# Reordering the fifth pair, one in-product of the next pairs, and some loads of an attention and feed-forward kernel

## The chip, the cores and the metric

The kernel runs on one core of one Trainium2 chip. The metric is the device time of one execution in microseconds (us), as the median of several runs; lower is better.

## The reference

Eight batches of eight heads of attention with a T5 bias, then a feed-forward block over the heads put side by side.

```python
scores = scale * np.matmul(q, k.transpose(0, 1, 3, 2))      # q, k, v: (8, 8, 576, 64)
scores = scores + bias.transpose(2, 0, 1)[None, :, :, :]    # a function of |i - j| and the head
scores = scores - np.max(scores, axis=-1, keepdims=True)
attn = np.exp(scores)
attn = attn / (np.sum(attn, axis=-1, keepdims=True) + 1e-09)
attn_out = np.matmul(attn, v)
...
x = attn_out.transpose(0, 2, 1, 3).reshape(B * S, H * D)    # (4608, 512)
h = x @ w_in                                                # w_in: (512, 2048)
g = np.maximum(0.01 * h, h)
return g @ w_out                                            # w_out: (2048, 512)
```

## The kernel before

The work of attention is cut into 32 pairs: pair n is batch n // 4 and two of its heads, `p = n % 4`. The feed-forward block is cut into nine blocks of 512 tokens; each has 16 in-products (four matmuls of 512 columns into one PSUM bank, then a leaky ReLU, `leaky`, on ScalarE or VectorE) and 16 quarters of out-products. These pieces are put between the steps of the pairs, so that TensorE has work while ScalarE and VectorE are at the attention. The order on each engine is the order in which the code is written (`manual_schedule`); semaphores are set by a framework, and so is the choice of a buffer within a pool.

The steps of a pair, by the names that the text uses:

- `transpose_q(n)`, `transpose_k(n)`: twelve (early pairs) or six transposes on TensorE into a bank of `ps_m`, then a copy to SBUF (L294 for q, L298 for k). From pair 9 on the transposes are made by DMA (`turn_by_dma`, L265) from rows that VectorE lays out (`pair_rows`, L257).
- `score(n, u)`: matmuls of keys and queries into one of the two buffers of `ps_s` (L316; u = 5, the last 64 keys, L319 and L320; u = 4, the edges, into `ps_o`, L309), then the exponential on ScalarE (L329, L336, L332). Below, third and fourth score are u = 2 and 3, fifth score is u = 5, and edge scores are u = 4.
- `band(n, u)`: VectorE multiplies the exponentials near the diagonal by the bias (L352).
- `av_tails(n)` and `av(n, e)`: the products with the values for head e (L365, L376), then `divide` on VectorE (reciprocal L385, product L387) into the tile `opair`. In later pairs `av_phase` (L411) does both heads in halves of the rows.
- `x_transposes(n)`: `opair` is turned into columns of `xT`, on TensorE (L437, copy L438) or by a DMA from SyncE's queue (L427).
- `piece_in` / `ffn_in` (L463, or L623 in halves) and `piece_out` / `ffn_out` (L504, L623): the pieces of the feed-forward block. `moe(k)` issues up to k in-products, `slot()` one, or two quarters, as planned for the pair.

The pool `ps_m` has two banks, which transposes and feed-forward pieces share.

Pairs 0 to 3 fill the pipeline with attention alone. Pair n = 4, the fifth, is written out by hand and has the first four in-products: one, two and one, at three places. Pairs 5 and 6 are pairs with only in-products (`room["only"]`), run by the general loop. From pair 8 on most pairs run `body_in_halves`.

Loads from HBM are issued on POOL's queue, in order. `load_qk(b, h0, h1)` brings q and k of some heads of a batch, `load_v_part` chunks of v, `load_w_in(half)` half of `w_in`. In the steady part `loads(n)` brings the next batch's data. It first has POOL copy one element of an earlier pair's `opair` (`tick`, L785), so that the loads behind it start only when that pair is divided:

```python
nc.gpsimd.tensor_copy(out=tick, in_=ops_[n - 2][0:1, 0, 0:1])
```

`loads(n)` with `p == 1` brings q and k of the next batch's upper heads and the first chunk of v.

Of the kernel before, what the change touches and what calls it, by code (L numbers as in the profile page):

```python
# [37 lines left out]
def kernel(  # L38
# [10 lines left out]
    nc = tc.nc  # L49

    B, H, S, D = q.shape
# [57 lines left out]
    def load_qk(b, h0, h1):  # L109
        i = b % NBUF  # L110
        for src, dst in ((q, qn[i]), (k, kn[i])):
            nc.gpsimd.dma_start(
                out=dst[0:RQ, h0:h1, :, :].rearrange("r h c d -> r h (c d)"),
                in_=src[b, h0:h1, :, :].rearrange("h (r c) d -> r h (c d)", c=NC),
            )

    def load_v_part(b, chunks, h0=0, h1=H):
        for c in chunks:
            nc.gpsimd.dma_start(  # L119
                out=vn[b % NBUF][:, c, h0:h1, 0:D],  # L120
                in_=v[b, h0:h1, c * P : (c + 1) * P, :].rearrange("h s d -> s h d"),
            )
# [56 lines left out]
    for j, (u, lo, w, m) in enumerate(groups):  # L179
# [5 lines left out]
        out=ub[:, C0 - BAND + 1 : C0],  # L185
# [42 lines left out]
    load_qk(1, 0, H // 2)  # L228
    load_v_part(0, range(NJ), 4, H)
    clear_v(nc.gpsimd, 1)  # L230
    load_qk(1, H // 2, H)

    def load_w_in(half):
        o = slice(half * (DF // 2), (half + 1) * (DF // 2))
        nc.gpsimd.dma_start(out=w_in_sb[:, :, o], in_=moe_w_in[:, o].rearrange("(c p) f -> p c f", p=P))
# [55 lines left out]
    def transpose_q(n):  # L291
        qt = qts[n] = qt_pool.tile([P, S], BF16, name="qt")
        copy = nc.scalar.copy if n <= n_pairs else nc.vector.tensor_copy
        copy(out=qt[:, 0:S].rearrange("p (r c) -> p r c", c=NC), in_=turned_pair(n, 0))  # L294

    def transpose_k(n):
        kt = kts[n] = kts_[n % 2]
        nc.vector.tensor_copy(out=kt[:, 0:S].rearrange("p (r c) -> p r c", c=NC), in_=turned_pair(n, 1))  # L298
        apart(kt)
# [69 lines left out]
    def av(n, e):  # L369
        b, p = items[n]  # L370
        at = at_[n % 2]
        ps = outs[n][e][:, 0 : (NJ + 1) * (D + 1)].rearrange("p (i d) -> p i d", d=D + 1)
        for ic in range(NJ + 1):
            for c in range(NJ):
                o = (e * NJ + c) * S + ic * P
                nc.tensor.matmul(ps[:, ic, :], lhsT=at[:, o : o + P], rhs=vn[b % NBUF][:, c, 2 * p + e, :],  # L376
                                 start=False, stop=(ic == NJ and c == NJ - 1))
        divide(n, (e,))
# [14 lines left out]
    def fence(sooner):  # L393

        f = nc.sync.nop(nofuse=True)  # L395
        tc.add_manual_dep(f.ins, sooner.ins.name, ended, reason="behind the last products of these rows")
        return f
# [243 lines left out]

    def body_in_halves(n, kinds):

        loads(n)
        turns = rows_ahead(n) if by_dma(n + 1) else []
        score(n, 0)
        av_tails(n - 1)
        last = fence(av_phase(n - 1, 0))
        score(n, 1)
        T, s = made["out"], at_piece["out"]  # L650
        if kinds[0] == "out":
            one, two = open_piece("out", (T, s)), open_piece("out", (T, s + 4))
        else:
            one, two = open_piece("in"), open_piece("out")
        phase = side_by_side(one, two)
        phase(0, 0, 1)
        av_phase(n - 1, 1, last)
        late_q = n == 2 * n_pairs
        if n + 1 < N and not late_q:
            transpose_q(n + 1)  # L660
        band(n, 0)
        divide(n - 1, range(2))
        if late_q:
            transpose_q(n + 1)
        last = fence(phase(0, 1, n_cc))
        score(n, 2)
        score(n, 3)
        phase(1, 0, n_cc, last)
        band(n, 1)
        if n + 1 < N:  # L670
            transpose_k(n + 1)
        score(n, 4)
        if kinds[0] == "in":
            one[2]()
        late = [n - 1]
        if x_by_dma(n - 1):
            x_transposes(late.pop())
        for m in turns:
            turn_by_dma(m)
        while stores:  # L680
            o, y = stores.pop(0)
            nc.sync.dma_start(out=o, in_=y)
        band(n, 2)
        if kinds[0] == "out":
            outs_pm[T] = one[0]
            ffn_out(T, s + 1)
            band(n, 4)
            score(n, 5)
            band(n, 5)
            ffn_out(T, s + 2)  # L690
            ffn_out(T, s + 3)
            for m in late:
                x_transposes(m, "o0")
                finished(m)
            outs_pm[T] = two[0]
            for part in range(5, 8):
                ffn_out(T, s + part)
            at_piece["out"] = (s + 8) % n_fc
            made["out"] += at_piece["out"] == 0
            return  # L700
        piece_out()
        band(n, 4)
        score(n, 5)
        band(n, 5)
        piece_out()
        piece_out()
        for m in late:
            x_transposes(m, "o1")
            finished(m)
        room["left"] -= 5  # L710
        moe(room["left"], 0)
# [56 lines left out]

    tick = per.tile([1, 1], BF16, name="tick")

    def loads(n):

        b, p = items[n]
        if n == 0:
            load_w_in(0)
            load_v_part(1, range(NJ))
            load_v_tail(1)
            load_w_in(1)
            load_w_out(0)
        elif n == 2:  # L780
            load_qk(2, 0, H // 2)
            load_w_out(1)
        if b < 1 or p < 1 or b > B - 2:
            return
        nc.gpsimd.tensor_copy(out=tick, in_=ops_[n - 2][0:1, 0, 0:1])  # L785
        if p == 1:
            load_qk(b + 1, H // 2, H)
            load_v_part(b + 1, (0,))
        elif p == 2:
            load_v_part(b + 1, (1, 2, 3))  # L790
        else:
            load_v_tail(b + 1)
            if b + 2 < B:
                load_qk(b + 2, 0, H // 2)
# [17 lines left out]
    def score(n, u):  # L812
        exp(n, u, qk_mm(n, u))
# [44 lines left out]
    n = n_pairs  # L858
# [2 lines left out]
    band(n - 1, 4)  # L861
    av_tails(n - 1)
    av(n - 1, 0)
    score(n, 2)
    av(n - 1, 1)
    score(n, 3)
    transpose_k(n + 1)
    x_transposes(n - 1)
    finished(n - 1)
    band(n, 0)  # L870
    band(n, 1)
    score(n, 5)
    room["left"] = 4
    moe(1)
    band(n, 2)
    transpose_q(n + 1)
    score(n, 4)
# [6 lines left out]
    for n in range(n_pairs + 1, N + 1):  # L884
        live = n < N
        more = n + 1 < N
        if x_by_dma(n - 2):
            finished(n - 2)
        plan(n)
        kinds = two_kinds(n)  # L890
        if kinds:
            body_in_halves(n, kinds)
            continue
        if live:
            begin(n)
            ps_a, ps_b = qk_mm(n, 0), qk_mm(n, 1)
            exp(n, 0, ps_a)
            exp(n, 1, ps_b)
        av_tails(n - 1)
        av(n - 1, 0)  # L900
        first = live and by_dma(n + 1)
        if first:
            band(n, 0)
        if more:
            transpose_q(n + 1)
        if live and not first:
            band(n, 0)
            turn_ahead(n)
        slot()
        av(n - 1, 1)  # L910
        if live and not room["only"]:
            band(n, 1)
        if more:
            transpose_k(n + 1)
        slot(True)
        if live:
            ps_a, ps_b, ps_c = qk_mm(n, 2), qk_mm(n, 3), qk_mm(n, 4)
            exp(n, 2, ps_a)
        x_transposes(n - 1)
        while stores:  # L920
            o, y = stores.pop(0)
            nc.sync.dma_start(out=o, in_=y)
        if not x_by_dma(n - 1):
            finished(n - 1)
        if not live:
            break
        if room["only"]:
            band(n, 1)
        band(n, 2)
        if room["only"]:  # L930
            if not by_dma(n + 2):
                pair_rows(n + 2)
            exp(n, 3, ps_b)
            moe(2)
            exp(n, 4, ps_c)
            score(n, 5)
            T, f = step("in")
            room["left"] -= 1

            def last_bands():  # L940
                band(n, 5)
                band(n, 4)

            leaky(T, f, ffn_in(T, f), True, last_bands)
            moe(room["left"])
            continue
        block = moe_block()
        next(block)
        exp(n, 3, ps_b)
        next(block)  # L950
        exp(n, 4, ps_c)
        if can("out"):
            next(block)
        band(n, 4)
        ps_a = qk_mm(n, 5)
        exp(n, 5, ps_a)
        band(n, 5)
        for _ in block:
            pass
# [31 lines left out]
```

## Time and profile before

| | |
|---|---|
| time, median of 3 runs | 372.75 us (372.66 to 373.42) |
| time of the profiled execution | 372.35 us |
| its span, first to last instruction | 370.6 us |
| granted TensorE clock | 1.000 |
| TensorE busy | 356.3 us (96%) |
| ScalarE busy | 245.4 us (66%) |
| VectorE busy | 192.9 us (52%) |
| POOL busy | 76.4 us (21%) |

All times below come from the one profiled execution. In a row of the timeline the first number is the start in us from the span's start, the second the duration of the group, then engine, line, operation, the tile written and the tile read, the shapes and the count; idle time before it and what ended it stand in brackets. PE is TensorE's matmuls, DVE is VectorE, ACT is ScalarE, SPq and POOLq are queues of DMA issues. Matmuls are pipelined: the next one starts long before the last one's end, so the distance between starts tells more than the duration.

### The profile page before, as it was taken

The page shows a single profiled execution, that of the slowest core. Times are in us where ns is not written, and L with a number is a line of the kernel's source. Part 1 is how long each engine was busy: PE and PEld are TensorE (multiplying, and loading weights), DVE is VectorE, ACT ScalarE, POOL GpSimd, SP SyncE. Part 2 cuts the span into 40 slices and gives each one's busy share as a digit, 9 for nine tenths or more (in the row PEclk, how much of TensorE's full clock was granted, in tenths as well). Part 3 has the DMA queues.
Part 4 walks back from the last instruction along what each step waited for, and adds up shares of the span by engine and source line. Part 5 has one row for each costly group of instructions (what it writes and reads, how often), then busy time and mean ns, then how long its engine had stood idle before and what let it go on. Part 6 is the DMA issues. An engine that isn't in the chain of part 4 may idle for free.

```text
span 370.6 us, 10507 instructions
## 1 busy us (share of the span) xinstructions
PE 356.3 (96%) x4453; PEld 187.7 (51%) x4496; DVE 192.9 (52%) x502; ACT 245.4 (66%) x382; POOL 76.4 (21%) x118
## 2 busy tenths in 40 slices
PE   6889999999999999999999999999999999999996
PEld 2455555555555555555555554555555544444443
DVE  4688687777757576666755566665553200200000
ACT  5998887478847787777877776777777365055111
POOL 8754431233023303330233023100000000000000
DMA  8999999999379989986799399532111000110122
GB/s 105 188 193 183 207 203 115 196 180 160 56 103 165 140 114 116 153 133 131 97 122 143 87 102 152 112 72 62 46 48 50 28 30 0 59 56 0 72 72 85
DMA packets 104358, 40.17 MB, mean 108 GB/s; under 512 B 83184, under 2 KB 98808, under 8 KB 104312
## 3 DMA queue, kind: packets, MB, share of 16 engines
q0 software_dynamic: 53696, 18.36, 50.9%
q1 hardware_dynamic: 49320, 19.06, 26.9%
q10 hardware_dynamic: 1296, 2.10, 1.5%
q8 instruction: 35, 0.57, 0.7%
q14 instruction: 11, 0.09, 0.1%
HBM read 37.68 MB, written 9.45 MB: 127 GB/s over the span
## 4 chain that ended last, share of the span: by engine, by line
PE 87%; ACT 4%; DMA 3%; DVE 3%; issue 2%; POOL 0%; ACTq 0%; DVEq 0%; POOLq 0%
PE pm L463 28%; PE pm L504 27%; PE pm L623 8%; PE ps_s L316 8%; PE ps_o L411 6%; PE ps_o L376 4%; DMA xT<-opair 2%; ACT at L329 2%; PE ps_s L319 2%; PE ps_o L365 1%; DVE opair L387 1%; PE ps_tx L437 1%; PE ps_q L309 1%; DMA kn<-in_k_dram 1%; PE pm L497 1%
## 5 line engine op out<-in xcount | busy, mean ns | idle before, releaser
L329 ACT ACTIVATE at<-ps_s 128x1024 bf16<-128x1024 f32 x128 | 124.6, 1028 | 25.6 <-PE ps_s L316 25.5
L476 ACT ACTIVATE gt<-pm 128x512 bf16<-128x512 f32 x138 | 82.9, 605 | 70.3 <-PE pm L463 69.4
L463 PE MATMUL pm<-xT,w_in_sb 128*128 128x512 bf16 x490 | 117.2, 379 | 1.1
L504 PE MATMUL pm<-w_out_sb,gt 128*128 128x512 bf16 x452 | 105.9, 379 | 3.3 <-issue 3.0
L352 DVE TENSOR_TENSOR at<-at,hk 128x768 bf16<-128x768 bf16 (+3 forms) x160 | 70.8, 454 | 58.0 <-ACT at L329 33.7
L463 PEld LDWEIGHTS <-w_in_sb 128*128 128x128 bf16 x508 | 47.8, 98 | 54.5 <-issue 0.7
L504 PEld LDWEIGHTS <-gt 128*128 128x128 bf16 x476 | 43.5, 98 | 49.5
L316 PE MATMUL ps_s<-qt,kt 64*128 64x512 bf16 x256 | 43.3, 380 | 3.6 <-ACT at L329 3.0
L623 PE MATMUL pm<-w_out_sb,gt 64*128 64x512 bf16 x168 | 42.2, 376 | 0.0
L517 DVE COPY y<-pm 128x512 f32<-128x512 f32 x28 | 19.4, 691 | 40.9 <-PE pm L504 38.1
L623 PE MATMUL pm<-xT,w_in_sb 64*128 64x512 bf16 x136 | 37.7, 376 | 0.4 <-DMA xT<-opair 0.4
L119 POOL DMA_DIRECT2D vn<-in_v_dram x32 | 29.9, 939 | 10.4 <-PE ps_s L316 8.1
L387 DVE TENSOR_TENSOR opair<-ps_o,rcp 128x320 bf16<-128x320 f32 x64 | 29.7, 488 | 1.6
L785 POOL COPY tick<-opair 1x1 bf16<-1x1 bf16 x18 | 3.5, 194 | 129.2 <-DVE opair L387 129.2
L411 PE MATMUL ps_o<-vn,at 64*128 64x65 bf16 x1520 | 29.5, 190 | 0.0
L411 PEld LDWEIGHTS <-at 64*128 64x128 bf16 x1520 | 27.1, 94 | 4.3 <-SPq L395 3.0
L316 PEld LDWEIGHTS <-kt 64*128 64x128 bf16 x256 | 11.6, 94 | 25.4 <-issue 16.5
L336 ACT ACTIVATE at<-ps_s 128x576 bf16<-128x576 f32 x32 | 21.8, 683 | 0.2 <-PE ps_s L320 0.2
L332 ACT ACTIVATE at<-ps_q 128x256 bf16<-128x256 f32 x64 | 21.4, 396 | 0.3 <-PE ps_q L309 0.2
L385 DVE RECIPROCAL rcp<-ps_o 128x5 f32<-128x5 f32 x64 | 10.0, 182 | 21.6 <-PE ps_o L376 18.3
L376 PE MATMUL ps_o<-vn,at 128*128 128x65 bf16 x520 | 20.1, 194 | 0.0
L376 PEld LDWEIGHTS <-at 128*128 128x128 bf16 x520 | 17.9, 98 | 3.5 <-issue 0.7
(66 smaller groups left out, 254.4 us busy)
## 6 DMA issues: line engine op xcount, KB each, us to landing
out_dram<-y SPq DMA_DIRECT2D x28, 256.0 KB, 3.6
qn<-in_q_dram POOLq DMA_DIRECT2D x14, 288.0 KB, 5.9
kn<-in_k_dram POOLq DMA_DIRECT2D x14, 288.0 KB, 7.0
vn<-in_v_dram POOLq DMA_DIRECT2D x28, 128.0 KB, 6.3
w_in_sb<-in_moe_w_in_dram POOLq DMA_DIRECT2D x2, 1024.0 KB, 12.4
w_out_sb<-in_moe_w_out_dram POOLq DMA_DIRECT2D x2, 1024.0 KB, 15.7
out_dram<-y ACTq DMA_DIRECT2D x7, 256.0 KB, 2.0
qn<-in_q_dram POOLq DMA_DIRECT2D x4, 144.0 KB, 4.4
```

The costliest lines, as they stand in the source:

```text
L119: nc.gpsimd.dma_start(out=vn[b % NBUF][:, c, h0:h1, 0:D], in_=v[b, h0:h1, c * P : (c + 1) * P, :].rearrange("h s d -> s h d"),)
L316: nc.tensor.matmul(ps[:, e, :], lhsT=kt[r, u * P : (u + 1) * P], rhs=qt[r, 0:512], start=True, stop=True)
L329: nc.scalar.activation(at[:, :, u, 0:512], ps, AF.Exp, scale=scale)
L336: nc.scalar.activation(at4[:, 0:S], ps.rearrange("p e i -> p (e i)")[:, 0:S], AF.Exp, scale=scale)
L352: nc.vector.tensor_tensor(out=o, in0=o, in1=m, op=ALU.mult)
L376: nc.tensor.matmul(ps[:, ic, :], lhsT=at[:, o : o + P], rhs=vn[b % NBUF][:, c, 2 * p + e, :], start=False, stop=(ic == NJ and c == NJ - 1))
L387: nc.vector.tensor_tensor(out=opair[:, :, e * D : (e + 1) * D], in0=ps[:, :, 0:D], in1=rcp.to_broadcast([P, NJ + 1, D]), op=ALU.mult)
L411: m = nc.tensor.matmul(outs[n][e][:, ic * (D + 1) : (ic + 1) * (D + 1)], lhsT=at[halves[r], o : o + P], rhs=vn[b % NBUF][halves[r], c, 2 * ...
L463: nc.tensor.matmul(pm, lhsT=w_in_sb[:, c, f * P : (f + 1) * P], rhs=xT[c][:, t0 : t0 + TT], start=(c == 0), stop=(c == n_cc - 1))
L476: nc.scalar.activation(g, pm, AF.Prelu, bias=0.0, scale=1.0, alpha=0.01)
L504: nc.tensor.matmul(pm, lhsT=gt[:, f, ts * P : (ts + 1) * P], rhs=w_out_sb[:, f, :], start=(f == 0), stop=(f == n_fc - 1))
L623: m = nc.tensor.matmul(pm, lhsT=w[halves[r]], rhs=x[halves[r]], start=(k == 0 and c == 0), stop=(low is not None and k == 1 and c == n_cc ...
```

## The change

Four edits. In the fifth pair both value products stand ahead of the third score, and the output transposes, the fifth score and the first in-product ahead of the key transposes. On POOL's queue the first half of `w_in` is loaded ahead of q and k of the upper heads of batch 1. In pairs 5 and 6 the first in-product stands behind the second value product. In `body_in_halves` a pair with `p == 1` (n = 9, 13, 17, 21, 25) calls `loads` after its division, and the tick reads the `opair` of pair n - 1 in place of n - 2.

```diff
     clear_v(nc.gpsimd, 1)
-    load_qk(1, H // 2, H)
...
     def body_in_halves(n, kinds):
-        loads(n)
+        late_loads = items[n][1] == 1
+        if not late_loads:
+            loads(n)
...
         if late_q:
             transpose_q(n + 1)
+        if late_loads:
+            loads(n, 1)
         last = fence(phase(0, 1, n_cc))
...
-    def loads(n):
+    def loads(n, behind_pair=2):
         b, p = items[n]
         if n == 0:
             load_w_in(0)
+            load_qk(1, H // 2, H)
             load_v_part(1, range(NJ))
...
-        nc.gpsimd.tensor_copy(out=tick, in_=ops_[n - 2][0:1, 0, 0:1])
+        nc.gpsimd.tensor_copy(out=tick, in_=ops_[n - behind_pair][0:1, 0, 0:1])
...
     av_tails(n - 1)
     av(n - 1, 0)
+    av(n - 1, 1)
     score(n, 2)
-    av(n - 1, 1)
     score(n, 3)
-    transpose_k(n + 1)
     x_transposes(n - 1)
     finished(n - 1)
+    score(n, 5)
     band(n, 0)
-    band(n, 1)
-    score(n, 5)
     room["left"] = 4
     moe(1)
+    transpose_k(n + 1)
+    band(n, 1)
     band(n, 2)
     transpose_q(n + 1)
     score(n, 4)
...
-        slot()
+        if not room["only"]:
+            slot()
         av(n - 1, 1)
+        if room["only"]:
+            slot()
```

## The prediction

> **What bounds the kernel now.** I read the page first: busy shares, then the chain that ended last.
>
> ```profile
> span 370.6 us, 10507 instructions
> ...
> PE 356.3 (96%) x4453; PEld 187.7 (51%) x4496; DVE 192.9 (52%) x502; ACT 245.4 (66%) x382; POOL 76.4 (21%) x118
> ...
> PE 87%; ACT 4%; DMA 3%; DVE 3%; issue 2%; POOL 0%; ACTq 0%; DVEq 0%; POOLq 0%
> ```
>
> TensorE is busy 96% of the span and 87% of the chain. A change is therefore worth what it adds to or takes from TensorE's idle time, so I went to the list of TensorE's waits for a wait that one of the four edits could touch, and found one in the steady part, late in the kernel:
>
> ```profile
> PE pm L623 <- DMA xT<-opair: 0.4, 1, 0.4
> ```
>
> The other edits lie in the fifth to seventh pairs (n = 4, 5, 6), and for these I read the timeline engine by engine. TensorE in the fifth pair:
>
> ```profile
> 31.08 0.39 PE L316 MATMUL ps_s<-qt,kt 64*128 64x512 bf16 x2
> 31.41 0.79 PE L376 MATMUL ps_o<-vn,at 128*128 128x65 bf16 x20
> 32.13 0.39 PE L316 MATMUL ps_s<-qt,kt 64*128 64x512 bf16 x2
> 32.45 0.45 PE L279 MATMUL ps_t<-ident,kn 96*64 96x96 bf16 x12
> 33.02 0.45 PE L437 MATMUL ps_tx<-ident,opair 128*128 128x128 bf16 x5
> 33.31 0.38 PE L319 MATMUL ps_s<-qt,kt 128*128 128x512 bf16 x1
> 33.53 0.19 PE L320 MATMUL ps_s<-qt,kt 128*128 128x64 bf16 x1
> 33.75 1.02 PE L463 MATMUL pm<-xT,w_in_sb 128*128 128x512 bf16 x3
> 34.70 0.45 PE L279 MATMUL ps_t<-ident,qn 96*64 96x96 bf16 x12
> 35.08 0.29 PE L309 MATMUL ps_q<-qt,kt 64*128 64x64 bf16 x8
> 35.46 2.75 PE L463 MATMUL pm<-xT,w_in_sb 128*128 128x512 bf16 x12
> 38.14 0.39 PE L316 MATMUL ps_s<-qt,kt 64*128 64x512 bf16 x2
> ```
>
> The columns are start and duration. The reader should see two things. The twelve in-product matmuls (three in-products of four) take 2.75 us though one takes 0.38: they start every (2.75 - 0.38) / 11 = 0.215 us, with no hole. And a change between tiles of 64 and of 128 rows costs about 0.1: the second value product starts 0.32 after the third score's two matmuls, which side by side need 0.215. VectorE and ScalarE beside them:
>
> ```profile
> 31.42 0.49 DVE L387 TENSOR_TENSOR opair<-ps_o,rcp 128x320 bf16<-128x320 f32 x1
> 32.25 0.20 DVE L385 RECIPROCAL rcp<-ps_o 128x5 f32<-128x5 f32 x1 [0.34 <-PE ps_o L376]
> 32.48 0.49 DVE L387 TENSOR_TENSOR opair<-ps_o,rcp 128x320 bf16<-128x320 f32 x1
> 32.94 0.76 DVE L298 COPY kt<-ps_t 128x576 bf16<-128x576 bf16 x1
> 33.73 0.23 DVE L286 TENSOR_TENSOR kt<-kt,own 128x128 bf16<-128x128 bf16 x1
> 33.87 0.45 DVE L438 COPY xT<-ps_tx 128x576 bf16<-128x576 bf16 x1
> 34.24 1.35 DVE L352 TENSOR_TENSOR at<-at,hk 128x512 bf16<-128x512 bf16 x3
> 35.51 0.75 DVE L294 COPY qt<-ps_t 128x576 bf16<-128x576 bf16 x1
> ```
>
> ```profile
> 29.88 3.78 ACT L329 ACTIVATE at<-ps_s 128x1024 bf16<-128x1024 f32 x4
> 33.82 0.65 ACT L336 ACTIVATE at<-ps_s 128x576 bf16<-128x576 f32 x1 [0.16 <-PE ps_s L320]
> 34.81 0.60 ACT L476 ACTIVATE gt<-pm 128x512 bf16<-128x512 f32 x1 [0.34 <-PE pm L463]
> ```
>
> In this order the key transposes go first, VectorE copies them (32.94) while TensorE is at the output transposes, and when the first in-product starts (33.75; one of its four records is missing) everything behind it is prepared.
>
> **Part 1, the fifth pair.** The instructions are the same; only their order changes. I take the rows' durations and walk through the new order.
>
> Without the third score between them the second value product starts at 31.0 and its last matmul at 31.6; the third score starts at 31.7 instead of 31.08 (20 products with one change of shape take 0.72: 31.41 to 32.13), the fourth 0.215 later. Two changes of shape are saved, 0.2. The reciprocal waits for VectorE's first division (31.42 + 0.49 = 31.91); to the end of the second division it is 0.72 (32.25 to 32.97), so 32.64. The output transposes start at 32.69, not 33.02 (0.05 after the division's end, as in the row): 0.33 better.
>
> Here the gain stops. One exponential of this shape takes 1.03 on the page, and ScalarE's four were back to back, one every (3.78 - 1.03) / 3 = 0.92:
>
> ```profile
> L329 ACT ACTIVATE at<-ps_s 128x1024 bf16<-128x1024 f32 x128 | 124.6, 1028 | 25.6 <-PE ps_s L316 25.5
> ```
>
> The second ends at 29.88 + 0.92 + 1.03 = 31.83, but the third score now ends only at 31.7 + 0.39 = 32.09. So the third exponential runs from 32.13 to 33.16 and the fourth ends at 34.08, 0.4 later than 29.88 + 3.78 = 33.66. The fifth score needs the third's bank: 33.21, instead of 33.31. The first in-product follows 0.24 later, at 33.45 instead of 33.75; its fourth matmul starts at 34.10 and ends at 34.48.
>
> Then the key transposes, now behind it (a matmul and a change of shape later, 34.41), and the query transposes (34.67: the twelve fill 0.45, of which the last one alone is 0.2). Both in-products and transposes share two banks of the pool `ps_m`. In the changed program the query transposes get the bank of the first in-product, so they wait until ScalarE has read it: fourth exponential to 34.08, the fifth score's 0.65 to about 34.65 (they overlap a little), the in-product's 0.60 to about 35.15, release 0.05: 35.2. TensorE stands from 34.67, for 0.5. The edge scores follow at +0.38 (34.70 to 35.08) and the second in-product at +0.38 (35.08 to 35.46, an upper bound, since that start was itself held by ScalarE's read ending at 35.41; 0.2 is the lower): 35.8 to 35.96, against 35.46. The key copy (34.86 + 0.76 = 35.65) is just ready.
>
> The second stall is new too. In the changed program the third in-product is put in the second's own bank, not the other one. It must wait for the second's four matmuls (3 x 0.215 + 0.38 = 1.03), ScalarE's 0.60 and two hand-overs of 0.05: 1.71 after its start, where the rows show 0.86. That is 0.85 more. The Trainium skill, Perfetto Trace Analysis, section "Optimizing Tensor Performance" (Matmuls), says that independent matmul groups should rotate through different banks so that the evacuation of one overlaps the next, which this order breaks. The row agrees: twelve matmuls without a hole where they did rotate. But rotation would save little here: the other bank is held by the query copy, which is now last on VectorE behind the key copy (to 35.65), the 0.23 product and two bands of 0.45 (to 36.8), so it ends at 37.5, and the third in-product would start at 37.55 instead of 37.5 to 37.7.
>
> From the third in-product's start to the fourth's it is 0.86, and from there to the next pair's first score 38.14 - (35.46 + 2 x 0.86) = 0.96: 39.3 to 39.5 against 38.14. **Cost: 1.15 to 1.4, taken as 1.28.** All of it is on the path: TensorE has nothing else queued, and the following pairs wait for nothing that runs by a clock of its own.
>
> **Part 2, w_in ahead of q and k of upper heads.**
>
> ```profile
> 21.40 0.75 POOL L235 DMA_DIRECT2D w_in_sb<-in_moe_w_in_dram  x1 [1.69 <-DMA qn<-in_q_dram]
> ```
>
> ```profile
> w_in_sb<-in_moe_w_in_dram POOLq DMA_DIRECT2D x1, 1024.0 KB, 11.5
> ```
>
> Before, w_in lands at 21.40 + 11.5 = 32.9, ahead of 33.45 too, so its coming earlier buys nothing. On POOL's queue w_in is moved past two DMAs and those two behind it; the same three follow each other, and whatever stands behind them keeps its place. So q and k now land where w_in did, near 32.9, and VectorE reads them for n = 6 only after its query copy, past 37.5: 4.6 us of cover. **Zero**; were that cover gone, each us of delay would stand before VectorE's next divisions.
>
> **Part 3, sixth and seventh pair.** The in-product moves behind the second value product; shapes are alike, so no change of shape is saved.
>
> ```profile
> 40.95 0.42 DVE L352 TENSOR_TENSOR at<-at,hk 128x512 bf16<-128x512 bf16 x1
> 41.39 0.20 DVE L385 RECIPROCAL rcp<-ps_o 128x5 f32<-128x5 f32 x1
> ```
>
> The value product ends four matmuls, 0.86, earlier, but the reciprocal is behind a band that ends at 41.37, so it gains 0.02 to 0.06. The in-product's read by ScalarE moves to just before the third exponential is due. **-0.05 a pair, -0.1 in all**, between -0.15 and 0.
>
> **Part 4, loads of q, k and v one pair later** (n = 9, 13, 17, 21, 25). The wait in TensorE's list:
>
> ```profile
> 214.28 0.18 POOL L785 COPY tick<-opair 1x1 bf16<-1x1 bf16 x1 [15.99 <-DVE opair L387]
> ```
>
> ```profile
> 214.65 1.21 SPq L427 DMA_TRANSPOSE xT<-opair  x1
> ```
>
> ```profile
> 223.90 0.37 PE L623 MATMUL pm<-xT,w_in_sb 64*128 64x512 bf16 x1 [0.39 <-DMA xT<-opair]
> ```
>
> ```profile
> xT<-opair SPq DMA_TRANSPOSE x1, 9.2
> ```
>
> ```profile
> xT<-opair SPq DMA_TRANSPOSE x1, 2.6
> ```
>
> The first landing is that of the transfer at 214.65 (n = 23), issued 0.4 after a tick that let q, k and v go; the second is that of n = 22, one pair earlier, with no such loads beside it. The product at 223.90 needs the first. It started 0.38 (a matmul) + 0.39 (idle) = 0.77 after its predecessor, where 0.215 would do: 0.55 is lost. With the tick on the same pair's `opair` the loads leave at about 224.2, the transfer of n = 23 lands near 217 to 219, and **0.55 goes**. Behind the tick on POOL stand only these loads and those of the next pair, and nobody waits for POOL otherwise. The loads now meet n = 24's transfer, whose rows no in-product needs before the batch is complete three pairs later. The other four places show no TensorE wait, so nothing is gained there.
>
> **Sum:** +1.28 + 0 - 0.10 - 0.55 = +0.63. The profiled execution took 372.35 (span 370.6, 1.75 around it), 0.4 under the median of 372.75, within the three runs' spread of 0.76. Added to the median: 373.4. 0.2% (0.75 us) is about what a measurement tells from no change.
>
> **The rivals.** *Late loads bring back what they took* (slower). Six loads now go at once beside the transposes of n = 24 and n = 28; the rows read from q and k must be there here:
>
> ```profile
> 239.00 0.35 DVE L257 COPY pr<-qn 96x768 bf16<-96x768 bf16 x1
> ```
>
> From 224.2 that leaves 14.8 us. If a load took longer VectorE would stand before `pr`, and the queries behind it, in up to five pairs. It decides from 15 us to landing; rows speak against it (a transfer among loads took 9.2). If it only cancels the 0.55: +1.2; with one stall more: +1.7, 373.95 to 374.45.
>
> *No stall in the fifth pair* (faster): if ScalarE is done in time and the banks rotate, the second in-product starts at 34.67 + 0.38 + 0.38 = 35.43, as before, and the rest follows without a hole; then -0.03 - 0.1 - 0.55 = -0.7, 372.05. The shared bank and the order on VectorE speak against it.
>
> *The delay is taken up later*: the Trainium skill, Perfetto Trace Analysis, section "Identifying the Most-Contended Engine", judges TensorE's headroom by its weight loads' busy share, not by that of matmuls; here 51%, which would leave room. In rows, as a mechanism: TensorE catches up in later pairs, as far as it stood idle there for other engines; half of the 1.28 made up gives 372.75. Against it speaks the 0.215 pitch without holes.
>
> **How the numbers follow.** Forecast 0.48, its own range +0.45 to +1.1 (373.2 to 373.85: part 1 at 1.15 to 1.45, part 3 at -0.15 to 0, part 4 at -0.55 to -0.35); of it 0.28 lies under 373.5 and 0.20 above. Late loads 0.21, all slower. No stall 0.20, half of it beyond 0.2%. Taken up 0.11. Within 0.2%: 0.28 + 0.10 + 0.11 = 0.49; slower 0.20 + 0.21 = 0.41; faster 0.10. The range, 372.1 to 374.3, leaves out the faster half of "no stall" and the worst late loads.
>
> **What would show it.** Right: TensorE idle before the query transposes of n = 4 (about 0.5) and between its second and third in-products (0.85), first score of n = 5 near 39.4, and no wait on `xT<-opair` near 224. Wrong: three in-products without a hole in n = 4, or a VectorE wait on `qn` or `kn` after n = 9.

## The result, and the profile after

| | before | after |
|---|---|---|
| median of 19 runs each | 372.49 us (371.77 to 374.05) | 373.39 us (372.86 to 374.01) |
| ratio to before, 95% interval | | 1.0023 (1.0015 to 1.0031) |
| profiled execution | 372.35 us | 373.38 us |
| its span | 370.6 us | 371.6 us |

The change makes the kernel slower by 0.86 us by the ratio, with an interval of 0.56 to 1.15 us. 373.4 was predicted and 373.39 measured. It was put within 0.2% of no change and came out just beyond, with an interval on both sides of that line. How much of the agreement is merit is the subject of what follows: one term of the sum was wrong, and another thing covered it.

The page of the changed kernel: span, busy time by engine, shares of the chain that ended last.

```profile
span 371.6 us, 10509 instructions
...
PE 356.8 (96%) x4455; PEld 187.9 (51%) x4496; DVE 193.8 (52%) x502; ACT 245.1 (66%) x382; POOL 75.7 (20%) x118
...
PE 90%; ACT 4%; DVE 3%; issue 2%; ACTq 0%; DVEq 0%
```

TensorE is still 96% busy and still the bound. The chain's 3% of DMA is gone. The list of TensorE's waits (total, times, longest) has no wait on `xT<-opair` any more, but has new ones:

```profile
PE ps_tx L436 <- DVE opair L386: 0.7, 2, 0.4
PE pm L462 <- ACT gt L475: 0.7, 1, 0.7
...
PE ps_t L278 <- ACT gt L475: 0.3, 1, 0.3
```

Where they lie is seen in TensorE's timeline of the fifth pair (start, duration; in brackets the idle time and what ended it). Line numbers in this part of the code are one less than before: L462 is the L463 of before.

```profile
30.33 0.67 PE L364 MATMUL ps_o<-v,at 64*128 64x65 bf16 x10
30.93 1.40 PE L375 MATMUL ps_o<-vn,at 128*128 128x65 bf16 x40
32.26 0.60 PE L315 MATMUL ps_s<-qt,kt 64*128 64x512 bf16 x4
33.15 0.45 PE L436 MATMUL ps_tx<-ident,opair 128*128 128x128 bf16 x5 [0.29 <-DVE opair L386]
33.77 0.38 PE L318 MATMUL ps_s<-qt,kt 128*128 128x512 bf16 x1 [0.16 <-ACT at L328]
33.98 0.19 PE L319 MATMUL ps_s<-qt,kt 128*128 128x64 bf16 x1
34.22 0.81 PE L462 MATMUL pm<-xT,w_in_sb 128*128 128x512 bf16 x3
34.96 0.45 PE L278 MATMUL ps_t<-ident,kn 96*64 96x96 bf16 x12
35.72 0.45 PE L278 MATMUL ps_t<-ident,qn 96*64 96x96 bf16 x12 [0.31 <-ACT gt L475]
36.10 0.29 PE L308 MATMUL ps_q<-qt,kt 64*128 64x64 bf16 x8
36.32 1.04 PE L462 MATMUL pm<-xT,w_in_sb 128*128 128x512 bf16 x4
38.04 1.89 PE L462 MATMUL pm<-xT,w_in_sb 128*128 128x512 bf16 x8 [0.69 <-ACT gt L475]
39.86 0.61 PE L315 MATMUL ps_s<-qt,kt 64*128 64x512 bf16 x4
40.30 0.32 PE L364 MATMUL ps_o<-v,at 64*128 64x65 bf16 x10
```

The reader should see the two holes, before the query transposes (35.72) and between the second and the third in-product (38.04). Both end with ScalarE's reading of an in-product (`gt`). ScalarE's own rows:

```profile
34.52 0.66 ACT L335 ACTIVATE at<-ps_s 128x576 bf16<-128x576 f32 x1
35.07 0.60 ACT L475 ACTIVATE gt<-pm 128x512 bf16<-128x512 f32 x1
36.48 0.66 ACT L331 ACTIVATE at<-ps_q 128x256 bf16<-128x256 f32 x2 [0.81 <-PE ps_q L308]
37.39 0.60 ACT L475 ACTIVATE gt<-pm 128x512 bf16<-128x512 f32 x1 [0.26 <-PE pm L462]
39.10 0.60 ACT L475 ACTIVATE gt<-pm 128x512 bf16<-128x512 f32 x1 [1.11 <-PE pm L462]
```

ScalarE waits for the second in-product until 37.39, reads it to 37.99, TensorE starts the third at 38.04, and then ScalarE stands 1.11 for that. The two engines take turns on one bank. The pool's other bank would have been no help: it holds the query transposes, and VectorE copies them, behind the key copy and two bands, until 37.32 + 0.75 = 38.07:

```profile
37.32 0.75 DVE L293 COPY qt<-ps_t 128x576 bf16<-128x576 bf16 x1
```

A pair is best measured from the start of its `ps_o<-v,at` (the first value product of the pair before) to the next such row. Before, these rows are

```profile
29.77 0.67 PE L365 MATMUL ps_o<-v,at 64*128 64x65 bf16 x10
...
38.58 0.32 PE L365 MATMUL ps_o<-v,at 64*128 64x65 bf16 x10
...
47.06 0.32 PE L365 MATMUL ps_o<-v,at 64*128 64x65 bf16 x10
...
55.52 0.31 PE L365 MATMUL ps_o<-v,at 64*128 64x65 bf16 x10
```

and after, for the next two pairs,

```profile
48.67 0.32 PE L364 MATMUL ps_o<-v,at 64*128 64x65 bf16 x10
57.10 0.31 PE L364 MATMUL ps_o<-v,at 64*128 64x65 bf16 x10
```

The fifth pair took 38.58 - 29.77 = 8.81 and takes 40.30 - 30.33 = 9.97: **+1.16**. Pairs 5 and 6 took 16.94 together and take 57.10 - 40.30 = 16.80: **-0.14**. From there to the end every pair has its old length to within 0.01, except the stretch with the wait on `xT`, called pair 25 below. Before:

```profile
221.11 0.32 PE L365 MATMUL ps_o<-v,at 64*128 64x65 bf16 x10
...
231.40 0.32 PE L365 MATMUL ps_o<-v,at 64*128 64x65 bf16 x10
```

After:

```profile
222.67 0.32 PE L364 MATMUL ps_o<-v,at 64*128 64x65 bf16 x10
...
232.39 0.32 PE L364 MATMUL ps_o<-v,at 64*128 64x65 bf16 x10
```

It took 10.29 and takes 9.72 (**-0.57**). And the fifth pair begins 30.33 - 29.77 = **0.56** later. The four add up to the 1.0 by which the spans differ. The first three were expected in about these sizes, the last was not expected at all.

### The profile page after: what moved, and what is told of

It is laid out like the page before. It is cut to its first block, busy times and chain, and to the rows that moved or that the text cites. A ratio compares the mean times of both kernels' runs of the same rounds, so it can differ in the third digit from the quotient of the medians.

```text
span 371.6 us, 10509 instructions
## 1 busy us (share of the span) xinstructions
PE 356.8 (96%) x4455; PEld 187.9 (51%) x4496; DVE 193.8 (52%) x502; ACT 245.1 (66%) x382; POOL 75.7 (20%) x118
## 4 chain that ended last, share of the span: by engine, by line
PE 90%; ACT 4%; DVE 3%; issue 2%; ACTq 0%; DVEq 0%
PE pm L462 28%; PE pm L503 27%; PE pm L622 9%; PE ps_s L315 8%; PE ps_o L410 6%; PE ps_o L375 4%; ACT at L328 2%; PE ps_s L318 2%; PE ps_o L364 1%; PE ps_w L766 1%; DVE opair L386 1%; PE ps_q L308 1%; PE ps_tx L436 1%; PE pm L496 1%; DVE at L351 1%
## 5 line engine op out<-in xcount | busy, mean ns | idle before, releaser
L462 PE MATMUL pm<-xT,w_in_sb 128*128 128x512 bf16 x492 | 117.3, 379 | 1.5 <-ACT gt L475 0.7
L462 PEld LDWEIGHTS <-w_in_sb 128*128 128x128 bf16 x508 | 47.6, 98 | 55.2 <-issue 1.7
L622 PE MATMUL pm<-xT,w_in_sb 64*128 64x512 bf16 x136 | 37.5, 376 | 0.0
L119 POOL DMA_DIRECT2D vn<-in_v_dram x32 | 28.0, 881 | 6.7 <-PE ps_s L319 3.4
```

The lines of the kernel that those rows point to most:

```text
L119: nc.gpsimd.dma_start(out=vn[b % NBUF][:, c, h0:h1, 0:D], in_=v[b, h0:h1, c * P : (c + 1) * P, :].rearrange("h s d -> s h d"),)
L462: nc.tensor.matmul(pm, lhsT=w_in_sb[:, c, f * P : (f + 1) * P], rhs=xT[c][:, t0 : t0 + TT], start=(c == 0), stop=(c == n_cc - 1))
L622: m = nc.tensor.matmul(pm, lhsT=w[halves[r]], rhs=x[halves[r]], start=(k == 0 and c == 0), stop=(low is not None and k == 1 and c == n_cc ...
```

## The experiments

The theory: the two holes of the fifth pair cost 1.16 and all comes from banks that wait for ScalarE; the in-products of pairs 5 and 6 give 0.14; w_in costs nothing; late loads give 0.55. The first four runs split the change into its parts. The runs of a group were compared with runs of the kernel before on the same chip.

**The order of the fifth pair alone.**

```diff
     av(n - 1, 0)
-    score(n, 2)
     av(n - 1, 1)
+    score(n, 2)
     score(n, 3)
-    transpose_k(n + 1)
     x_transposes(n - 1)
     finished(n - 1)
-    band(n, 0)
-    band(n, 1)
     score(n, 5)
+    band(n, 0)
     room["left"] = 4
     moe(1)
+    transpose_k(n + 1)
+    band(n, 1)
     band(n, 2)
```

> Only the new order of the fifth pair. Theory (two waits on shared banks in the fifth pair, nothing taken up later): from its first 40-product value run to the next pair's first score the pair takes 8.9 us as in the changed kernel (7.8 before), the late wait on xT near 224 us stays, and the time is +1.1 us, ratio 1.003. Rival (taken up later): the pair takes 8.9 us but the time is +0.6 or less, ratio 1.0015. Rival (the fifth pair is innocent, the start-up before it is what grew): pair within 0.3 us of before.

Measured: 373.96 us against 372.38, ratio 1.0044 (1.0022 to 1.0067), fifth pair 9.97, both holes, every pair behind it as before but pair 25, which takes 9.72 although its loads are issued early (more below); the wait that was expected to stay is not there. 1.16 us would be a ratio of 1.0031, inside the interval. So the whole loss is in this edit.

**The late loads alone.**

```diff
-        loads(n)
+        late_loads = items[n][1] == 1
+        if not late_loads:
+            loads(n)
...
+        if late_loads:
+            loads(n, 1)
...
-in_=ops_[n - 2][0:1, 0, 0:1]
+in_=ops_[n - behind_pair][0:1, 0, 0:1]
```

> Only the later loads. Theory: no TensorE wait on xT<-opair near 224 us, transfer of n = 23 lands in 2.6 to 4 us, time -0.55 us, ratio 0.9985. Rival (late loads bring back what they took): a VectorE or TensorE wait appears after n = 9, ratio 1.000 or above.

Measured: 372.51 against 372.38, ratio 1.0008 (0.9986 to 1.0031). In its profile pair 25 takes 9.72, as it should, and no pair is longer. But the median does not show the 0.55, which would be a ratio of 0.9985.

**All but the fifth pair**, the whole change with the old order of that pair.

> The whole change without the new order of the fifth pair. Theory: -0.55 from the loads and -0.1 to -0.2 from the in-product of pairs 5 and 6, ratio 0.998. Rival (w_in's place lengthens the start-up by 0.5 us): ratio 0.9995.

Measured: 372.50 against 372.38, ratio 1.0002 (0.9983 to 1.0020). Fifth pair 8.81; pairs 5 and 6 take 8.37 and 8.43 (8.48 and 8.46 before), so the -0.14 belongs to the in-product behind the second value product. Pair 25 takes 9.71. Yet the span is 370.6, as before, where -0.7 had to be seen: its fifth pair begins at 30.53, 0.76 later than in the first profile, which takes back what the pairs gain.

**w_in ahead of q and k alone.**

```diff
-    load_qk(1, H // 2, H)
...
             load_w_in(0)
+            load_qk(1, H // 2, H)
```

> Only w_in ahead of q and k of the upper heads. Theory: w_in lands some 2 to 3 us earlier, TensorE waits nowhere longer, ratio 1.000 within 0.0005. Rival: the start-up to the fifth pair's first value product (30.4 us before, 30.9 in the changed kernel) is 0.5 us longer, ratio 1.0015.

Measured: 372.74 against 372.38, ratio 1.0003 (0.9982 to 1.0025). The fifth pair and all after it keep their lengths, except pair 25. The fifth pair begins at 30.99, 1.22 later than in the first profile, where the rival had 0.5; the last section traces that to a slow beginning and a wait before 16 us, ahead of the moved load. And here is what broke the theory: in this kernel, and in the one with the fifth pair alone, the loads of q, k and v are issued early as before, and yet pair 25 takes 9.72 and TensorE does not wait for `xT`. The wait that part 4 was to remove is not there when nothing removes it.

**The kernel before once more**, for a second profile.

> The kernel before once more, nothing edited, for a second profile of it. Theory (the wait of 0.55 us on xT near 224 us and the start-up of 29.77 us in its first profile are chance of transfer times): the wait on xT is absent or of another size, the xT transfer of the pair lands in under 9.2 us, and the start of the fifth pair's value products falls anywhere from 29.8 to 31. Rival (both belong to the kernel): the wait is again 0.5 to 0.6 us and the start-up within 0.1 us of 29.77.

Measured: 372.48 us, span 370.7. No wait on `xT`, pair 25 takes 9.72, and the fifth pair begins 0.69 later than in the first profile:

```profile
30.46 0.67 PE L365 MATMUL ps_o<-v,at 64*128 64x65 bf16 x10
```

The time from issue to landing of the pair's transfer, in this profile and in four others with early loads (second profile of before, fifth pair alone, w_in alone, and two kernels told below: values first, exchange alone):

```profile
xT<-opair SPq DMA_TRANSPOSE x1, 8.3
```

```profile
xT<-opair SPq DMA_TRANSPOSE x1, 7.2
```

```profile
xT<-opair SPq DMA_TRANSPOSE x1, 7.1
```

```profile
xT<-opair SPq DMA_TRANSPOSE x1, 7.9
```

```profile
xT<-opair SPq DMA_TRANSPOSE x1, 8.7
```

In the first profile it was 9.2. In the first profile TensorE needed the tile 223.90 - 0.55 - 214.65 = 8.70 after the issue, and the program around it is the same in all six. So among six executions one is late by 0.5, one meets the need to within 0.02, and four are early by 0.4 to 1.6. With late loads it lands after 2.6, with 6 us to spare. Part 4 removes a wait that comes now and then; on average over the six it is worth (0.57 + 0.02) / 6 = 0.1, an estimate from few executions.

**The third in-product in another bank.** Now to the cause of the holes. In the changed kernel, the third in-product of the fifth pair takes its bank from the pool of the scores:

```diff
+        elif spare == "s":
+            pm = ps_s_pool.tile([P, 512], FP32, name="pm1", tag="ps_s")
...
-    moe(2)
+    moe(1)
+    moe(1, "s")
```

> The changed kernel, but the third in-product of the fifth pair goes into a bank of the score pool instead of into the bank where the second one still waits for ScalarE. Theory (the fifth pair is longer because successive in-products sit in one PSUM bank): the hole of 0.69 to 0.85 us between second and third in-product goes, the pair falls from 9.97 to between 9.1 and 9.3 us (8.81 before), and the time falls by about 0.8 us against the changed kernel, to about 0.4 over the kernel before. Rival (the hole is only where a wait for ScalarE's gelu shows, and ScalarE's queue of exponentials and gelus is the bound there): the hole moves to the score or the transposes that follow, and the pair stays within 0.2 us of 9.97.

Measured: 372.63 against 372.71, ratio 0.9993 (0.9982 to 1.0005).

```profile
29.99 0.67 PE L364 MATMUL ps_o<-v,at 64*128 64x65 bf16 x10
...
35.38 0.45 PE L278 MATMUL ps_t<-ident,qn 96*64 96x96 bf16 x12 [0.31 <-ACT gt L477]
...
35.98 2.76 PE L464 MATMUL pm<-xT,w_in_sb 128*128 128x512 bf16 x12
...
39.12 0.31 PE L364 MATMUL ps_o<-v,at 64*128 64x65 bf16 x10
```

The twelve matmuls run without a hole again, and the pair takes 39.12 - 29.99 = 9.13, which is 0.84 less. ScalarE's rows show the cadence restored, one reading every 0.86 to 0.87 in place of a gap of 1.71 (37.39 to 39.10):

```profile
37.05 0.60 ACT L477 ACTIVATE gt<-pm 128x512 bf16<-128x512 f32 x1 [0.25 <-PE pm L464]
37.92 0.60 ACT L477 ACTIVATE gt<-pm 128x512 bf16<-128x512 f32 x1 [0.27 <-PE pm L464]
38.78 0.60 ACT L477 ACTIVATE gt<-pm 128x512 bf16<-128x512 f32 x1 [0.27 <-PE pm L464]
```

The rival, that ScalarE's queue is the bound there, is out: the same ScalarE work fits once TensorE may go on. The time is lower than the 0.4 over the kernel before that was expected. That figure left out what the other edits give: with +0.32 for the fifth pair, -0.13 for pairs 5 and 6 and -0.1 for pair 25, the sum is +0.1, inside the interval.

**The query transposes in another bank too.**

```diff
-        ps = ps_m_pool.tile([P, 8 * P], BF16, name="ps_t", tag="m")
+        if n == n_pairs + 1 and j == 0:
+            ps = ps_s_pool.tile([P, 8 * P], BF16, name="ps_t", tag="ps_s")
+        else:
+            ps = ps_m_pool.tile([P, 8 * P], BF16, name="ps_t", tag="m")
```

> As the run before, and the query transposes of the fifth pair also go into a bank of the score pool, so that they need not wait for ScalarE's gelu of the first in-product. Bank theory: the hole of 0.31 to 0.48 us before the query transposes goes as well, and the pair ends between 8.7 and 9.0 us, about as before. Rival: the same as for the run before; or the two tiles taken out of the score pool make the scores wait for the exponentials, which would show as a wait of TensorE on a score tile and a pair of over 9.2 us.

Measured: 372.20 against 372.71, ratio 0.9985 (0.9973 to 0.9997).

```profile
30.32 0.67 PE L367 MATMUL ps_o<-v,at 64*128 64x65 bf16 x10
...
34.96 0.45 PE L281 MATMUL ps_t<-ident,kn 96*64 96x96 bf16 x12
35.24 0.42 PE L281 MATMUL ps_t<-ident,qn 96*64 96x96 bf16 x12
...
35.81 2.76 PE L467 MATMUL pm<-xT,w_in_sb 128*128 128x512 bf16 x12
...
38.95 0.31 PE L367 MATMUL ps_o<-v,at 64*128 64x65 bf16 x10
```

The first hole is gone as well: 38.95 - 30.32 = 8.63, another 0.50 less and 0.18 under the kernel before. The scores wait no longer for the two banks taken from them: the only wait on a score tile in this pair is the 0.16 that the changed kernel has too. The order of the changed kernel is no worse than the old one; the banks that it leads to are.

**Only the value products ahead of the third score** (the first two edits of the fifth pair, on the kernel before).

> The kernel before with one edit: in the fifth pair both value products stand ahead of the third score, k transposes, w_in and loads stay where they were. Theory (the move of the value products costs nothing, what costs is that k transposes and in-product changed places): the pair is 8.5 to 8.8 us against 8.81, and the time within 0.3 us of the kernel before. Rival (the later third score starves ScalarE's exponentials and so delays the pair): the pair is over 9.1 us and the time 0.3 to 0.5 us longer.

Measured: 372.42 against 372.71, ratio 0.9983 (0.9970 to 0.9997).

```profile
32.15 0.67 PE L365 MATMUL ps_o<-v,at 64*128 64x65 bf16 x10
...
40.75 0.32 PE L365 MATMUL ps_o<-v,at 64*128 64x65 bf16 x10
```

The pair takes 8.60, so this half of the order gains 0.21. Its profiled execution began the pair at 32.15, of which more below; its span of 372.2 therefore says nothing on the edit.

**Only the exchange of key transposes and first in-product.**

> The kernel before with one edit of the fifth pair: the k transposes and the first in-product change places, the third score stays between the value products. If the two parts of the fifth pair add up, the exchange alone costs what the whole costs and the 0.21 us that the value products gained: 9.97 - 8.60 = 1.37 over 8.81, so a pair of 10.1 to 10.2 us and a time 1.2 to 1.4 us over the kernel before, with both holes (before the query transposes and between second and third in-product). Rival (the holes come of the two together, since the value products first bring the gelu of the first in-product late): the pair is 9.5 us or less, with one hole or none.

Measured: 373.64 against 372.49, ratio 1.0035 (1.0023 to 1.0047).

```profile
30.32 0.67 PE L365 MATMUL ps_o<-v,at 64*128 64x65 bf16 x10
...
35.82 0.45 PE L279 MATMUL ps_t<-ident,qn 96*64 96x96 bf16 x12 [0.31 <-ACT gt L476]
...
38.14 1.89 PE L463 MATMUL pm<-xT,w_in_sb 128*128 128x512 bf16 x8 [0.69 <-ACT gt L476]
...
40.40 0.32 PE L365 MATMUL ps_o<-v,at 64*128 64x65 bf16 x10
```

The pair takes 10.08: +1.27, with the same two holes of the same size. The loss is in this exchange, and the value products take 0.11 of it back. So the rival, that the holes come only of both parts together, is out.

**All but the exchange**: values first, the in-products of pairs 5 and 6, w_in first and late loads.

> The kernel before with all of the change but the exchange in the fifth pair: both value products ahead of the third score, the in-product of pairs 5 and 6 behind the second value product, w_in ahead of q and k, late loads; the k transposes stay ahead of the in-products. By adding up what the runs so far gave: fifth pair 8.60 (8.81 before), pairs 5 and 6 together 16.8 (16.93 before), no xT wait, so 0.35 us less than the kernel before, 0.2 to 0.9 under it by the median. Rival (the gain of the values first is lost when the loads move): the fifth pair is 8.8 or longer and the time as before.

Measured: 372.53 against 372.49, ratio 1.0001 (0.9987 to 1.0015). Its profile shows every length that was expected (fifth pair 8.59, pairs 5 and 6 16.78, pair 25 9.72), and its span of 370.2 is 0.4 shorter. The times do not show it: the median is not the 0.2 to 0.9 lower that was expected, though a gain of 0.35 lies inside the interval. Of all versions only two have an interval that ends below 1: the one with both banks and the one with the values first, each by a ratio of 0.9997 at its upper end.

## Why the prediction came out as it did

*Fifth pair: right, in mechanism, places and size.* Shifted by the 0.56 by which the pair begins later, the changed kernel's rows stand beside the walk through the new order thus:

| | predicted | measured - 0.56 |
|---|---|---|
| output transposes | 32.69 | 33.15: 32.59 |
| key transposes | 34.41 | 34.96: 34.40 |
| query transposes, held by ScalarE | 35.2 | 35.72: 35.16 |
| second in-product | 35.8 to 35.96 | 36.32: 35.76 |
| third in-product | 37.5 to 37.7 | 38.04: 37.48 |
| first score of the next pair | 39.3 to 39.5 | 39.86: 39.30 |

The cost is 1.16, at the lower end of 1.15 to 1.4; I took 1.28. (The range of the whole sum used 1.45, where the walk gives no more than 39.5 - 38.14 = 1.36; nothing hung on it.) The 0.12 between them is mostly one step: the edge scores were followed by the second in-product after 0.22 (36.10 to 36.32), near the lower bound of 0.2, where I took the middle to 0.38, 0.29. Most of the rest is the 0.04 by which the query transposes start earlier. That the later start of the third score sets ScalarE back, and with it the first in-product's release, was also right: the output transposes' gain stopped at the fifth score, as worked out.

The Trainium skill, Perfetto Trace Analysis, section "Optimizing Tensor Performance" (Matmuls), would have successive groups rotate through banks. The two runs with other banks agree with it and price it: 0.84 for the one, 0.50 for the other. My remark that rotation would save little was on the other bank of the same pool. That was not tried, but the row of the query copy bears it out: the copy ends at 38.07, which is 37.51 after the shift, where 37.5 was worked out, so that bank was no earlier free than the one that was taken (38.04). It took banks of another pool to close the holes.

*"No stall in the fifth pair"* is refuted by the two holes, *"taken up later"* by the lengths: not one of the later pairs became shorter because the fifth was longer. The Trainium skill, Perfetto Trace Analysis, section "Identifying the Most-Contended Engine", would judge the headroom by the weight loads' busy share (beside the share of the peak FLOPs); that is 51% here, and this delay found no room in it.

*w_in: zero, as said.* The load is moved from 20.3 to 22.3 us to 17.5 to 18.6 us on POOL's queue, and the rows `ps_o<-v,at` tell what that did: from the second of them (20.2 to 21.4) to the fourth, the start of the fifth pair, it is 9.59 to 9.61 in all six profiles with `w_in` ahead and in five of the six with it behind. The sixth, values first, takes 10.95, at a lower granted clock (last section). What stood behind kept its place but not its time: the second half of `w_in` was issued at 28.60 and is at 31.39, and no wait of TensorE comes of it.

*Pairs 5 and 6:* -0.14 instead of -0.1, within the bounds. It lies mostly in pair 5 (-0.11 and -0.03), not evenly. The way is the one described: pair 5's second reciprocal starts 43.00 - 40.30 = 2.70 after the pair, where it was 41.39 - 38.58 = 2.81; it gained 0.11, not 0.02 to 0.06.

*Late loads: this step failed.* The reading of the row was right, and the late loads do what I said (landing after 2.6, no wait). The mistake was to count a wait on a transfer, seen in one execution, as part of every execution. Beside the row stood what should have warned me: the tile was late by 0.5 after a transfer of 9.2, so a transfer 6% shorter has no wait. It should have been entered at something between 0 and -0.55; the six profiles say -0.1. The rival for it, that late loads bring back what they took, is refuted: no pair is longer, and VectorE nowhere waits for `qn` or `kn` of the steady part. It does wait near 240 us, for the DMA transpose of a coming pair's rows (`tu`), 0.3 in the changed kernel and 1.4 in the one with all but the fifth pair, but there the pairs keep their lengths.

With that the sum would have been 1.16 - 0.14 - 0.1 = +0.9, and the times say +0.86. I had +0.63 and added it to a median of three runs that was 0.26 above the later one of nineteen. Two errors of about a quarter of a microsecond cancelled; the 373.4 owes its last digits to that.

## What to carry to other kernels

Before two pieces of work change places, write down which buffer each takes and who still reads it: the exchange moved no work and lost 1.27 us, since it put groups of matmuls into a bank still being read while the pool's only other bank was no earlier free, and two banks of another pool gave nearly all of it back (with the values first, 9.97 fell to 8.63, against 8.60 without the exchange). A wait on a transfer in one profile is a sample, not a constant: compare the slack with the spread of landing times, from a second profile of the same kernel if there is one, before it goes into a sum. With effects of some tenths, lengths of stages in the trace (equal to 0.02 here) tell more than the times, but only from a mark behind the part that varies.

## What was not expected of the hardware

The beginning is not reproducible, the rest is. In twelve profiles the start of the fifth pair's first value product lies between 29.77 and 32.15 us, in two profiles of the same kernel at 29.77 and 30.46, while the 27 pairs behind it repeat their lengths to about 0.02 us wherever no edit touches them and no transfer is late. The traces show where the difference is made. The first score starts at 6.64 to 7.21; in the changed kernel the whole 0.56 is already there. TensorE's first matmuls are slow, and in this profile for longer: the first twelve transposes of q take 0.69, against 0.45 in the first profile of the kernel before, at a granted clock of 1.00 in both. What ends the slow stretch stays open. From the first to the second row `ps_o<-v,at` it is 5.36 to 6.30; the two longest, 6.06 (the second profile of the kernel before) and 6.30 (w_in alone), are those in which VectorE stood longest for the load of the bias, 3.8 and 4.0, before 16 us, while `w_in` is issued at 17.5 at the earliest. And the 32.15 of the values-first run is mostly clock: between 21 and 25 us its granted clock was 0.57, where the first profile has 1.00, and the stretch from the second to the third such row took 6.85 instead of 5.5.

A transfer of the same rows through SyncE's queue took 2.6 us alone (in all six profiles with late loads) and 7.1 to 9.2 us among loads issued just before and after it, in six profiles with the same program around it.
